# A state-space convolution and a token mixer on one core: another division of the convolution's work among the engines, four product buffers in its last step, and an order for each step

## The chip, the cores and the metric

The kernel runs on one core of one Trainium2 chip. A core has a matrix engine (TensorE, PE in the profile, whose weight loads are listed apart as PEld), a vector engine (VectorE, DVE), a scalar engine (ScalarE, ACT), a general engine (GpSimd, POOL) and an engine that here only issues transfers (SyncE, SP). Each works through its own instructions in program order and waits on semaphores for the others. The metric is the device time of one execution in microseconds, lower being better.

## The reference

The input u has 2048 positions of 512 channels. Two residual blocks follow each other, each on a layer norm of its input:

```python
def _A_ref(u, log_A_real, A_imag, C_real, C_imag, log_dt, D_skip):
    dt = jnp.exp(log_dt)
    A = -jnp.exp(log_A_real) + 1j * A_imag
    C = (C_real + 1j * C_imag) * dt[:, None]
    P = jnp.exp((A * dt[:, None])[:, :, None] * pos[None, None, :])
    K = 2.0 * jnp.einsum("dn,dnl->dl", C, P).real
    y = jnp.fft.irfft(jnp.fft.rfft(u_t, 2 * L) * jnp.fft.rfft(K, 2 * L), 2 * L)[:, :, :L]
    return y + u * D_skip
...
h = x + _A_ref(_layernorm(x), ...)
h2 = h + _B_ref(_layernorm(h), B_x, B_w1, B_w2, B_w3, B_w4)
```

The first block is a causal convolution of each channel with a kernel K of 2048 taps, which is a sum of 128 decaying oscillations. The second is a mixer: a layer norm, w1, a gelu, four shifts along the positions, w2, a residual, and then an MLP with w3 and w4.

## The kernel before, in words

There are two phases. `conv_phase` computes the first block, `mixer_phase` the second. The mixer's instructions stand in an order written out by hand; its layers 1 to 4 appear in the profile as matmuls into l, l3a to l3g and acc. The change doesn't touch the mixer.

**The convolution** goes in four steps s of 128 channels each (`WID`), and the channels in 32 chunks g of 16 (`CH`), eight to a step. For each chunk `table(g)` builds the taps as an outer form. Phases of the oscillations are integers that POOL adds up (`phases`, tile pt). ACT turns them into an absolute value, a sine and a cosine (three passes over 128 x 1056). The decays are tables: E (from eb) for the short distances, ec for multiples of 512, and from these amx (DVE, kept in PSUM, with or without squares by ACT) and amy, tile amp (an outer product of E and ec, on DVE or POOL). Six products of phases and decays give the tables cs and sn: four are always on DVE (with amx), and the last part of each, csy and sny (with amp), is on DVE or POOL. `taps(s, g)` multiplies cs and sn on PE, and ACT copies the taps to kt.

`spectra_of_taps` transforms the taps of a step: 64 channels at once with transposes on DVE (`stage_a_turn`) or 32 at a time with ACT copies (`stage_a_taps`). `stage_a_x` does the same for the normalised input. For each of eight parts e of the spectrum, `product(s, e)` then takes a matmul with the table tbs (`stage_b`), multiplies the spectra (DVE, or ACT and POOL in two halves) into a buffer u, and, where the lists say so, adds the four terms pairwise to two on DVE or POOL. `stage_b_inv(s, e)` transforms back with the table ms, from two terms if they were added and from four if not, and ACT copies the result to at. `stage_a_inv` turns a quarter of it on DVE into one of the same two buffers u, transforms it with fis and adds it to h. In the last step `last_a_inv` does that in place. The tables of step s+1 are built while the products of step s run; the last step has only its products. The input's spectra of steps 2 and 3 are made early and parked in DRAM (`FAR`, `spectrum_x`, `back`).

**The order** of all this is worked out before the program is emitted, by a list scheduler (`Plan`). Each operation is a node with an engine, an estimated cost, what it reads and writes, and a nominal due time `at`. `order()` walks through time and for each engine takes what can start first, breaking near ties by the due time that follows from the node's successors. The due times come from `NOM`, a dictionary of numbers, and from `TS`, one start for each step. So they act as priorities, not as times. Where `order()` expects PE to be idle for long it puts in filler matmuls of the identity (`busy`), as many as its model of the clock asks for; their results are not used.

**The division** among engines is `SHARE`. 'amy', 'csy', 'sny' list the chunks (modulo 8) whose part is on POOL, 'sq' those with squares on ACT, one list for step 0 and one for all others. 'turn' lists the groups of 64 channels that are transposed (only the first list is read), 'hadd' the halves of a step whose addition to h is done by PE (only the first is read; a group is 2s + r//2 with s up to 2), 'mul0' and 'mul2' the products on POOL, 'sum0' to 'sum3' the pairwise sums on DVE and on POOL. 'nrm' lists the tiles of the first layer norm that POOL normalises; of the others the first `LND` are DVE's and the rest ACT's. `LNA` tiles would have their statistics from ACT instead of DVE.

**The start.** `rates()` makes the decays with nine exponentials on ACT from one PSUM bank: six for eb at once, three for ec later, between two loads of the activation tables. `transpose(t)` brings the parameters of 128 channels into place, `params` prepares them, `norm_x` is the layer norm of the input.

## Time and profile before

| | |
|---|---|
| Median of 3 runs | 686.98 us (686.71 to 688.92) |
| The profiled execution | 687.03 us |
| Its span, first to last instruction | 685.2 us |
| Mean granted PE clock | 0.994 |
| Busy share of the span | PE 95%, PEld 74%, DVE 80%, ACT 59%, POOL 59% |
| First weight matmul of the mixer (l) | 305.4 us |

The page cuts the span into 40 equal slices; each digit is a busy share in tenths (the granted clock for PEclk):

```profile
PE   5987989999999997999999999999999999999997
DVE  5998898999898998999978798866879954455554
ACT  7889878867889876245634555544365443444330
POOL 1889589968999999002676219355635555554210
PEclk9998999999999999999999999999999999999999
```

The mixer begins in slice 18. Up to slice 16 three engines are near full at once; afterwards PE alone is. All instructions that were emitted through the scheduler or the ordering wrapper carry one line, L86, so groups are told apart by their tiles. A group's row gives the line, engine and operation, the tiles written and read, their shapes, the count, then busy time and mean ns, then idle time of the engine before them and what ended it. An f32 matmul appears as two records.

### The profile page before, as it was taken

The numbers are of one execution on the slowest core, as the hardware profiler recorded it, in microseconds if no ns is written. First come the engines' busy times: TensorE is split into PE (matmuls) and PEld (weight loads), VectorE is DVE, ScalarE is ACT, GpSimd is POOL, SyncE is SP. The second block draws the span as 40 slices with busy tenths as digits, with TensorE's granted clock in tenths as the row PEclk, the third lists the DMA queues.
The fourth block names the chain that finished last, engine by engine and source line by source line (L and its number), as shares of the span: only waits on it lengthen the run. The fifth ranks groups of instructions, "written<-read, shape, count | busy, mean of one in ns | idle before, by whom it ended". The sixth has DMA issues, their size and how long they took to land.

```text
span 685.2 us, 16971 instructions
## 1 busy us (share of the span) xinstructions
PE 649.8 (95%) x6898; PEld 509.3 (74%) x6898; DVE 547.8 (80%) x952; ACT 407.6 (59%) x706; POOL 405.3 (59%) x422
## 2 busy tenths in 40 slices
PE   5987989999999997999999999999999999999997
PEld 5984756663677684768888888888888888888885
DVE  5998898999898998999978798866879954455554
ACT  7889878867889876245634555544365443444330
POOL 1889589968999999002676219355635555554210
PEclk9998999999999999999999999999999999999999
DMA  8940644011201133020232311134311342211004
GB/s 204 255 163 2 186 156 110 3 48 33 64 3 49 34 96 109 1 64 1 61 94 51 104 32 48 45 90 113 101 36 50 101 127 62 61 47 47 22 10 123
DMA packets 49266, 51.50 MB, mean 75 GB/s; under 512 B 6436, under 2 KB 33060, under 8 KB 49188
## 3 DMA queue, kind: packets, MB, share of 16 engines
q1 hardware_dynamic: 47524, 47.80, 24.7%
q10 hardware_dynamic: 1152, 1.57, 0.9%
q0 software_dynamic: 512, 1.05, 0.6%
q8 instruction: 54, 0.88, 0.5%
q14 instruction: 24, 0.20, 0.1%
HBM read 35.72 MB, written 8.39 MB: 64 GB/s over the span
## 4 chain that ended last, share of the span: by engine, by line
PE 61%; DVE 14%; ACT 12%; DMA 4%; POOL 4%; issue 3%; SPq 1%; DVEq 0%; ACTq 0%; POOLq 0%
PE l L86 24%; PE acc L86 11%; ACT pt L86 7%; PE bank L86 6%; DVE u L86 4%; DVE at L86 3%; PE l3g L86 3%; PE l3d L86 3%; PE l3f L86 3%; PE l3e L86 3%; PE l3c L86 3%; PE l3b L86 3%; PE l3a L86 3%; DMA h<-in_A_u_dram 3%; DVE cs L86 2%
## 5 line engine op out<-in xcount | busy, mean ns | idle before, releaser
L86 ACT ACTIVATE pt<-pt 128x1056 f32<-128x1056 int32 x64 | 69.8, 1091 | 14.7 <-DVE cs L86 6.6
L86 POOL TENSOR_TENSOR pt<-p,s 128x512 int32<-128x512 int32 x64 | 72.4, 1148 | 4.5 <-DVE sn L86 3.3
L86 PE MATMUL bank<-at,tbs 128*64 128x128 f32 (+1 forms) x768 | 63.1, 311 | 3.3 <-DVE u L86 1.6
L86 PEld LDWEIGHTS bank<-at,tbs 128*64 128x64 f32 x768 | 44.6, 134 | 20.6 <-ACT at L86 3.0
L86 PEld LDWEIGHTS bank<-ident 128*128 128x128 f32 x418 | 50.5, 199 | 8.3 <-issue 5.1
L86 PE MATMUL bank<-ident 128*128 128x128 f32 x418 | 54.6, 287 | 0.0
L86 PE MATMUL bank<-u,ms 64*128 64x128 f32 x768 | 50.5, 280 | 3.5 <-DVE at L86 1.3
L86 PEld LDWEIGHTS bank<-u,ms 64*128 64x128 f32 x768 | 45.3, 187 | 8.3 <-issue 1.8
L86 POOL TENSOR_TENSOR cs0w<-raw,cs0w 128x512 fp32r<-128x512 f32 x7 | 9.1, 1294 | 58.9 <-ACT cs0w L86 58.9
L86 DVE TENSOR_TENSOR cs<-pt,amx 128x512 f32<-128x512 f32 x64 | 40.9, 678 | 2.4 <-ACT pt L86 1.2
L86 DVE TENSOR_TENSOR h<-h,l 128x512 f32<-128x512 f32 x48 | 32.1, 684 | 11.1 <-PE l L86 11.1
L86 PEld LDWEIGHTS bank<-cs 128*32 128x32 f32 x1024 | 24.2, 111 | 21.9 <-POOL cs L86 6.1
L86 POOL TENSOR_TENSOR sn1w<-raw,sn1w 128x512 fp32r<-128x512 f32 x7 | 9.5, 1361 | 52.2 <-ACT sn1w L86 52.2
L86 PE MATMUL bank<-cs 128*32 128x64 f32 x1024 | 32.7, 225 | 7.8 <-DVE cs L86 3.6
L86 DVE TENSOR_TENSOR u<-u,l3f 128x512 f32<-128x512 f32 x14 | 9.5, 682 | 36.9 <-PE l3f L86 36.9
L86 ACT COPY at<-bank 128x512 f32<-128x512 f32 x40 | 25.0, 631 | 22.6 <-PE bank L86 22.6
L86 ACT ACTIVATE pt<-pt,halfpi 128x1056 f32<-128x1056 f32 x32 | 38.1, 1190 | 0.5
L86 POOL TENSOR_TENSOR sn<-pt,amp 128x512 f32<-128x512 f32 x30 | 36.8, 1228 | 1.4 <-ACT pt L86 1.1
L86 DVE STREAM_TRANSPOSE at<-bank 128x512 f32<-128x512 f32 (+1 forms) x40 | 35.6, 919 | 2.0 <-PE bank L86 1.9
L86 ACT ACTIVATE u<-u 128x512 f32<-128x512 f32 x56 | 35.4, 632 | 1.8
L86 PE MATMUL bank<-sn 128*32 128x64 f32 x1024 | 32.0, 223 | 2.5 <-DVE sn L86 2.5
L86 POOL TENSOR_TENSOR cs<-pt,amp 128x512 f32<-128x512 f32 x26 | 31.9, 1225 | 3.5 <-PE bank L86 1.2
(1157 smaller groups left out, 2085.1 us busy)
## 6 DMA issues: line engine op xcount, KB each, us to landing
raw<-in_B_w_dram SPq DMA_DIRECT2D x28, 256.0 KB, 2.8
xq<-xq SPq DMA_DIRECT2D x72, 64.0 KB, 2.0
h<-in_A_u_dram SPq DMA_DIRECT2D x32, 128.0 KB, 4.3
h<-in_A_u_dram SPq DMA_DIRECT2D x16, 256.0 KB, 4.4
rawa<-in_B_w_dram SPq DMA_DIRECT2D x14, 256.0 KB, 2.9
rawb<-in_B_w_dram SPq DMA_DIRECT2D x14, 256.0 KB, 2.8
ms<-in_mm_dram SPq DMA_DIRECT2D x4, 768.0 KB, 10.5
out_dram<-h SPq DMA_DIRECT2D x48, 64.0 KB, 1.7
```

Source lines behind the costliest of these rows:

```text
L86: ins = f(*args, **kw)
```

## The change

Only the convolution is touched.

- The lists: 'amy', 'csy', 'sny' and 'sq' now have one entry for each step. On POOL stand afterwards 23 amy (19 before), 26 csy (26) and 24 sny (30); 24 chunks have squares on ACT (22). One group of step 1 (index 2) goes from `stage_a_turn` to two pairs of `stage_a_taps`. Step 0 adds up its terms for e = 4, 6 on POOL (before 1, 4, 6 on POOL and 3 on DVE), step 2 for 4 on DVE and 3, 6 on POOL (4, 5, 6 on POOL), step 3 for 0, 1, 4, 6, 7 on DVE and 2, 5 on POOL, and not for 3 (all on DVE). Product 4 of step 3 is POOL's.
- The first layer norm: POOL normalises no tile, DVE 0 to 3, ACT 4 to 15. The statistics of tiles 0 to 3 are ACT's, by two passes each with an accumulated sum.
- The decays: ec for 512 comes from an exponential right after the six for eb, that for 1024 is its square (ACT), that for 1536 the product of both (POOL). The second visit to the exponential's table is gone. The evacuation of block 0's parameters goes to DVE.
- The last step has four product buffers: the two u and the space of thp and ini, the parameters that no table needs any more by then.
- The due times: most entries of `NOM` have an addend for each step now (`nom`), each step's start `TS` has its own, all values are new, and two empty nodes stand for the norm that follows the convolution.

```diff
--- before.py
+++ after.py
@@ -21,20 +21,20 @@
...
-SHARE = {'nrm': [[1], [5]], 'mul0': [[0], [7]], 'mul2': [[6], []], 'amy': [[0, 1, 3, 4, 5, 6, 7], [1, 2, 3, 6]], 'csy': [[1, 4, 5, 6, 7], [0, 1, 2, 3, 4, 5, 7]], 'sny': [[1, 2, 3, 5, 6, 7], [0, 1, 2, 3, 4, 5, 6, 7]], 'sq': [[0, 1, 5, 7], [0, 2, 3, 4, 6, 7]], 'turn': [[1, 2, 3, 5, 6, 7], [2, 3, 5, 6, 7]], 'hadd': [[0, 1, 2, 7], [0, 1, 2, 3, 5, 6, 7]], 'sum0': [[3], [1, 4, 6]], 'sum1': [[], [0]], 'sum2': [[], [4, 5, 6]], 'sum3': [[0, 1, 2, 3, 4, 5, 6, 7], []]}
+SHARE = {'nrm': [[], []], 'mul0': [[2], [7]], 'mul2': [[7], [4]], 'amy': [[0, 1, 2, 3, 4, 5, 6, 7], [0, 1, 2, 3, 4], [0, 1, 2, 4, 7], [3, 4, 5, 6, 7]], 'csy': [[2, 3, 5, 6], [0, 1, 2, 3, 4, 5, 6, 7], [0, 1, 2, 3, 4, 5, 6, 7], [0, 1, 2, 4, 5, 7]], 'sny': [[1, 2, 3, 5, 6, 7], [1, 2, 4, 6, 7], [0, 1, 2, 4, 6], [0, 1, 2, 3, 4, 5, 6, 7]], 'sq': [[0, 1, 2, 6], [0, 2, 3, 4, 5, 6, 7], [1, 2, 3, 4, 5, 6, 7], [1, 3, 4, 5, 6, 7]], 'turn': [[1, 3, 5, 6, 7], [2, 3, 5, 6, 7]], 'hadd': [[0, 1, 2], [0, 1, 2, 3, 5, 6, 7]], 'sum0': [[], [4, 6]], 'sum1': [[], [0]], 'sum2': [[4], [3, 6]], 'sum3': [[0, 1, 4, 6, 7], [2, 5]]}
...
-LND = 5
-LNA = 0
+LND = 4
+LNA = 4
...
@@ -333,6 +333,8 @@
     TS = [NOM["t0"]]
     for w_ in WID:
         TS.append(TS[-1] + NOM["per"] * w_ / 128)
+    TS = [t + NOM.get(f"t.{i}", 0) for i, t in enumerate(TS)]
+    nom = lambda n, s: NOM[n] + NOM[f"{n}.{s}"]
...
-    decays += [(ec[:, :, k], 512.0 * k) for k in range(1, 4)]
+    decays += [(ec[:, :, 1], 512.0)]
...
-        for i, (d, m) in enumerate(decays[:6]):
-            add("ACT", 0.52, lambda d=d, m=m: act.activation(d, plan.view(p), AF.Exp, scale=-m), r=["lam"], w=["eb", ("exp", i)], at=-93)
-        sine = lambda: act.activation(tiny, halfpi, AF.Sin)
-        add("ACT", 1.45, sine, r=[("exp", i) for i in range(6)], w=["trig"], at=-92)
+        for i, (d, m) in enumerate(decays):
+            add("ACT", 0.99 if i == 6 else 0.52, lambda d=d, m=m: act.activation(d, plan.view(p), AF.Exp, scale=-m), r=["lam"],
+                w=["ex" if i == 6 else "eb", ("exp", i)], at=-93, frees=p if i == 6 else None)
+        add("ACT", 1.45, lambda: act.activation(tiny, halfpi, AF.Sin), r=[("exp", i) for i in range(7)], w=["trig"], at=-92)
 
         def rest():
-            for i, (d, m) in enumerate(decays[6:]):
-                add("ACT", 0.99 if i else 2.3, lambda d=d, m=m: act.activation(d, plan.view(p), AF.Exp, scale=-m), r=["lam"], w=["trig"], at=NOM["exp"])
-            add("ACT", 1.45, sine, w=["trig", "ex"], at=NOM["exp"], frees=p)
+            add("ACT", 0.99, lambda: act.activation(ec[:, :, 2], ec[:, :, 1], AF.Square), w=["ex"], at=NOM["exp"])
+            add("POOL", 1.2, lambda: gp.tensor_tensor(ec[:, :, 3], ec[:, :, 1], ec[:, :, 2], ALU.mult), w=["ex"], at=NOM["exp"])
...
+            if t:
+                act.activation(blk(thp, t, 1), chunked(b[:, 0:128]), AF.Copy, scale=1.0 / TWO_PI)
+            else:
+                v.tensor_scalar(blk(thp, t, 1), chunked(b[:, 0:128]), 1.0 / TWO_PI, None, ALU.mult)
+            copy = act.copy if t else v.tensor_copy
+            copy(am[:, t * 128 : t * 128 + 128], b[:, 128:256])
+            copy(blk(ini, t, 1), chunked(b[:, 256:384]))
+
+        add("ACT" if t else "DVE", 0.54 if t else 0.6, evac, r=[("prm", t)], w=[("A", t), ("C", t), ("I", t)], frees=p)
...
-        if g % 8 in SHARE["sq"][g >= 8]:
+        if g % 8 in SHARE["sq"][g // 8]:
...
-        pooled = lambda n: ("POOL", 1.04 if n == "amy" else 1.18, gp) if g % 8 in SHARE[n][g >= 8] else ("DVE", dve(CH * 32), v)
+        pooled = lambda n: ("POOL", 1.04 if n == "amy" else 1.18, gp) if g % 8 in SHARE[n][g // 8] else ("DVE", dve(CH * 32), v)
...
-        nominal = NOM["kg0"] + c * NOM["kgs0"] if s == 0 else TS[s - 1] + NOM["kg"] + c * NOM["kgs"] * WID[s - 1] / WID[s]
+        nominal = NOM["kg0"] + c * NOM["kgs0"] if s == 0 else TS[s - 1] + nom("kg", s) + c * nom("kgs", s) * WID[s - 1] / WID[s]
...
     g_ = [t.rearrange("p (d i t) -> p d i t", i=32, t=2) for t in uu]
+    uu += [t.rearrange("p g i d -> p (g i d)") for t in (thp, ini)]
+    PARAM = [("A", t) for t in R4] + [("I", t) for t in R4]
+
+    def turn_of(s, e):
+
+        k = e % (4 if s + 1 == NS else 2)
+        return uu[k], [("u", k)] + (PARAM if k > 1 else [])
...
-        u, uk = uu[e % 2], ("u", e % 2)
+        u, uk = turn_of(s, e)
...
-            add("ACT", 0.22 + n * 0.51e-3, lambda: act.copy(tap, taps_()), w=[uk], frees=p)
-            add("POOL", 3.0, pooled, r=keys, w=[uk, ("made", s, e)])
+            add("ACT", 0.22 + n * 0.51e-3, lambda: act.copy(tap, taps_()), w=uk, frees=p)
+            add("POOL", 3.0, pooled, r=keys, w=uk + [("made", s, e)])
         else:
-            add("DVE", 0.07 + 2 * n * 1.06e-3, mult, r=keys, w=[uk, ("made", s, e)], frees=p)
+            add("DVE", 0.07 + 2 * n * 1.06e-3, mult, r=keys, w=uk + [("made", s, e)], frees=p)
...
-        q = uu[e % 2][:, 0 : 2 * n].rearrange("p (i k d) -> p i k d", i=4, k=2)
+        u, uk = turn_of(s, e)
+        q = u[:, 0 : 2 * n].rearrange("p (i k d) -> p i k d", i=4, k=2)
...
-        a0 = 16 - LNA
-        for j in range(a0):
+        for j in range(LNA, 16):
             add("DVE", 0.6, lambda j=j: v.bn_stats(bx[:, j, :], h[:, j, :]),
                 r=[("x", j // 2, c) for c in R4], w=[("bs", j)])
-        for j in range(a0):
+        for j in range(LNA, 16):
             add("DVE", 0.08, lambda j=j: v.bn_aggr(mv[:, j, :], bx[:, j, :]), r=[("bs", j)], w=["mv"])
...
+            for j in range(LNA):
                 add("ACT", 0.62, lambda j=j: act.activation(junk, h[:, j, :], AF.Copy, accum_out=sm[:, j : j + 1]),
-                    r=[("x", j // 2, c) for c in R4], w=[("u", 0), "sm"])
...
+    add("DVE", 0.4, lambda: None, r=["part"], w=["mv"], at=TS[NS])
+    add("DVE", 2.75, lambda: None, r=["mv"], w=["norm"], at=TS[NS])
     plan.filler = busy
     plan.run()
```

In the same way as in `taps`, every `NOM` of 'kg', 'kgs', 'ak', 'ax', 'b', 'ib', 'y' and 'ys' is replaced by `nom` of that step.

46 lines of the change are left out of this document (21 added, 25 removed).

## The prediction

> **What bounds the kernel now.** I read the chain that ended last first (start, length, what), to see where the span is set.
>
> ```profile
> core 0 of [0], span 685.2 us
> 305.40 8.63 PE l L86 x36
> ...
> 675.33 5.45 PE l L86 x24
> ```
>
> From 305.4 us on the chain is TensorE (PE) alone, and the change touches nothing there: those 379.8 us stay. Whatever happens, happens in the convolution before 305.4. So I cut that part into stretches. The columns are length, then busy time (instructions) of PE, PEld, DVE, ACT and POOL, then the granted clock, DMA share and GB/s.
>
> ```profile
> 0.00:30.00 30.00, 22.27 (x174) 21.52 (x174) 22.90 (x71) 22.89 (x46) 13.59 (x25) 1.00 0.84 207
> 30.00:51.00 21.00, 18.07 (x320) 17.28 (x316) 19.96 (x43) 18.87 (x29) 18.06 (x18) 1.00 0.57 211
> 51.00:69.00 18.00, 14.15 (x284) 8.76 (x282) 15.30 (x22) 16.28 (x31) 17.91 (x16) 0.81 0.01 2
> 69.00:137.00 68.00, 63.24 (x1438) 45.33 (x1430) 62.39 (x104) 56.87 (x103) 56.76 (x57) 1.00 0.39 115
> 137.00:206.00 69.00, 64.57 (x1122) 40.22 (x1121) 65.72 (x105) 53.86 (x94) 57.20 (x60) 1.00 0.15 37
> 206.00:264.00 58.00, 53.51 (x1377) 40.09 (x1377) 52.22 (x74) 50.27 (x88) 55.49 (x53) 1.00 0.24 66
> 264.00:294.00 30.00, 28.30 (x414) 19.34 (x403) 27.42 (x42) 9.54 (x17) 9.52 (x8) 1.00 0.14 37
> ...
> 0.00:305.40 305.40, 274.38 (x5238) 199.61 (x5238) 276.18 (x484) 232.22 (x411) 228.54 (x231) 0.99 0.31 89
> ```
>
> PE looks fullest, but part of it is filler: matmuls of the identity that carry no result. The same view of the tile ident alone (PE, PEld, POOL):
>
> ```profile
> 69.00:137.00 68.00, 5.30 (x38) 4.54 (x38) 0.00 (x0) 1.00 0.39 115
> 137.00:206.00 69.00, 10.25 (x50) 6.18 (x50) 0.00 (x0) 1.00 0.15 37
> 206.00:264.00 58.00, 5.28 (x24) 3.05 (x24) 0.00 (x0) 1.00 0.24 66
> 264.00:294.00 30.00, 2.29 (x15) 1.90 (x16) 0.00 (x0) 1.00 0.14 37
> ```
>
> Taken off, PE's own work is 57.9 of 68 us, 54.3 of 69, 48.2 of 58 and 26.0 of 30, against 62.4, 65.7, 52.2 and 27.4 on DVE. DVE is the bound in three of these stretches; between 206 and 264 POOL (55.5) is a little above it. From 30 to 264 DVE is idle for 18.4 us in all (lengths less busy time: 1.0, 2.7, 5.6, 3.3, 5.8). Work taken off DVE should therefore come out nearly whole, unless PE or POOL is next.
>
> **The change part by part.** The rows for DVE, with busy time and mean ns of one, then idle time before it and its releasers:
>
> ```profile
> L86 DVE TENSOR_TENSOR u<-xs,bank 128x1024 f32<-128x1024 f32 x23 | 27.6, 1214 | 0.8 <-ACT xs L86 0.6
> L86 DVE TENSOR_TENSOR sn<-pt,amx 128x512 f32<-128x512 f32 x32 | 21.7, 679 | 3.8 <-ACT pt L86 1.5 <-POOL h L86 1.3 <-ACT amx L86 0.5
> L86 DVE STREAM_TRANSPOSE at<-bank 128x512 f32<-128x512 f32 x24 | 16.0, 697 | 0.0
> L86 DVE TENSOR_TENSOR amx<-E,amx 128x512 f32<-128x512 f32 x22 | 15.1, 686 | 5.8 <-ACT amx L86 5.6
> L86 DVE TENSOR_TENSOR amx<-E,amx 128x896 f32<-128x896 f32 x10 | 11.0, 1098 | 2.7 <-ACT amx L86 2.7
> L86 DVE BATCH_NORM_STATS2 bs<-h 128x6 f32<-128x512 f32 x16 | 10.5, 666 | 0.0
> L86 DVE TENSOR_TENSOR amp<-E,ec 128x512 f32<-128x512 f32 x13 | 10.2, 788 | 0.1
> L86 DVE TENSOR_TENSOR u<-u 128x256 f32<-128x256 f32 x18 | 7.7, 470 | 0.3
> L86 DVE TENSOR_TENSOR cs<-pt,amp 128x512 f32<-128x512 f32 x6 | 6.5, 1079 | 0.0
> L86 DVE TENSOR_TENSOR sn<-pt,amp 128x512 f32<-128x512 f32 x2 | 2.2, 1118 | 0.0
> L86 DVE TENSOR_SCALAR scratch<-scratch 128x128 f32<-128x128 f32 x4 | 0.9, 220 | 0.1
> ```
>
> The new lists move the following on DVE, stage by stage.
>
> The tables of step 0 (0 to about 69 us): four tiles' statistics go to ACT, 4 x 0.666 = -2.66 (their short aggregates are left aside); one amp more goes to POOL, -0.79; one cs comes back, +1.08; the three evacuations of block 0 come from ACT. No row shows those three on DVE; 0.22 each as the nearest row, twice that as the other end: +0.7. Sum -1.7.
>
> The tables of step 1, with the products of step 0: amp -0.79, cs -1.08, three sn back at +1.12 = +3.35, one more chunk that squares on ACT -0.41 (1.098 - 0.686), one pair of sums (e=3) gone, -0.94, and one group of tap spectra built without transposes, 4 x 0.697 = -2.79. Sum -2.7.
>
> The tables of step 2: -0.79 - 1.08 + 3.35 - 0.41 = +1.1. Of step 3: amp -0.79, cs +1.08, a pair of sums from POOL +0.94 = +1.2. The products of step 3: one product to POOL, -1.21, three pairs of sums gone from DVE, -2.82, together -4.0. In step 2 the pooled product is only another one, and the extra index 7 in the old list hadd has no group (indices end at 5), so its removal does nothing.
>
> The price of sn is the soft one: 0.68 (the same size with an operand amx) to 1.12; I take 1.12, the row of the operation itself. At 0.68 the whole would be 2.6 us better.
>
> The last step is not DVE's alone. Its PE work, first and last row of PE's timeline between the first product and the first matmul of what follows:
>
> ```profile
> 275.95 1.10 PE L86 MATMUL bank<-at,tbs 128*64 128x128 f32 x16
> ...
> 293.91 0.59 PE L86 MATMUL bank<-h,ident 128*128 128x512 f32 x1
> ```
>
> That is 18.0 us, of which at most 2.3 us were filler. And PE gains work from the lists; these rows price it:
>
> ```profile
> L86 PE MATMUL bank<-u,ms 64*128 64x128 f32 x768 | 50.5, 280 | 3.5 <-DVE at L86 1.3 <-DVE u L86 1.2 <-POOL u L86 0.6
> L86 PE MATMUL bank<-kt,fas 32*32 32x512 f32 x192 | 11.8, 600 | 1.9 <-DVE at L86 1.6 <-ACT at L86 0.3
> L86 PE MATMUL bank<-fas,kt 32*64 32x32 f32 x512 | 8.7, 219 | 0.0
> ```
>
> A product without its sums needs 16 more of the first row, 16 x 50.5/768 = 1.05: two in step 0, one in the last. The group that is no longer transposed goes from 11.8/6 = 1.97 to 8.7/2 = 4.35, +2.4. So PE's own work becomes 57.9 + 2.1 + 2.4 = 62.4 of 68 in the stretch from 69 us (it still fits), and 26.0 + 1.05 = 27.05 of 30 in the last. The last stretch can give at most 30 - 27.05 = 2.95. What would let it give so much are the four buffers: now steps 2's transposes hold both u, and the first product (273.5) waits for them. If the products still start where they do, PE needs 18.0 - 2.3 + 1.05 = 16.75 from there, a gain of 1.2. Between the two I take 2.0.
>
> POOL and ACT:
>
> ```profile
> L86 POOL TENSOR_TENSOR sn<-pt,amp 128x512 f32<-128x512 f32 x30 | 36.8, 1228 | 1.4 <-ACT pt L86 1.1 <-POOL pt L86 0.2
> L86 POOL TENSOR_TENSOR amp<-E,ec 128x512 f32<-128x512 f32 x19 | 21.4, 1130 | 5.5 <-DVE ec L86 5.1
> L86 POOL TENSOR_SCALAR h<-h,mvh,bs 128x512 f32<-128x512 f32 x2 | 4.1, 2070 | 0.0
> L86 ACT ACTIVATE h<-h,bs 128x512 f32<-128x512 f32 x10 | 7.4, 800 | 0.0
> L86 ACT ACT_TABLE_LOAD x4 | 5.1, 1283 | 0.8 <-PEq L1640 0.7
> L86 ACT ACTIVATE ec<-bank 128x512 f32<-128x512 f32 x3 | 3.2, 1150 | 0.0
> ```
>
> POOL loses two normalised tiles (-4.14) and six sn (-7.37), gains four amp (+4.52), a product in two halves (about two sn, +2.46) and the cube of the decay (about an amp, +1.1): -3.4 in all. Normalising on POOL also made DVE wait once, 1.3 us (the sn row above); with no tile on POOL I take that off: -1.3.
>
> ACT at the start: two exponentials become one square (-1.15), and the return to the exponential's table goes (two loads, -2.57). It gains eight passes for the statistics. No row has one with an accumulated sum; 8 x 0.80 = +6.4 as the nearest, plus two tiles to normalise, +1.6. The net, about +4.3, meets 7.1 + 2.1 us of ACT idle time before 51 us, so I cost it at nothing; if these passes stand ahead of the first tables' sines in ACT's order, it costs the part that the loads don't pay back, 6.4 - 3.7 = 2.7.
>
> **The sum.** -1.7 - 2.7 + 1.1 + 1.2 - 2.0 - 1.3 = -5.4, and 687.03 (the profiled execution, 1.8 us over its span of 685.2; the median of the runs, 686.98, is the same) becomes 681.6. Ends: with the last stretch at 2.95 and sn at 0.68, -9.0 (678.0); with 1.2 there and ACT's 2.7 paid, -1.9 (685.1). The new priorities are costed at nothing for themselves: they decide the rivals.
>
> **The rivals.**
>
> *The order also takes DVE's waits.* Each step gets its own numbers. If half of the 18.4 us of idle time goes too, 681.6 - 9.2 = 672.4. For it: the idle time is in many small waits of about 1 us. Against: PE, at 62.4 of 68, leaves little in one stretch, POOL in another.
>
> *The last step gives nothing more, because POOL's two pairs of sums stand in DVE's way.* DVE's cs with amp takes 1.079 while POOL is at work, against 0.68 with amx, which lies in PSUM. If the last step stays as it is (0 for 2.0, and e=3 costs its 1.05), 687.03 - 3.4 + 1.05 = 684.7. For it, in a page's words: the Trainium skill, "SBUF — State Buffer", Who interferes with whom, says that a DVE instruction with two SBUF inputs contends with a GpSimd one that reads SBUF, one of them blocking for its whole length. These rows agree. Against: DVE falls to 14 of 18 us there (18.0 less 4.0), so it has room.
>
> *ACT takes DVE's place.*
>
> ```profile
> DVE amx L86 <- ACT amx L86: 8.3, 13, 1.2
> ```
>
> This wait (us, times, longest) is DVE's largest, and ACT gets more in its way. If it grows by two thirds, 5.5 us, the gain is gone: 687.1. Against: ACT has 11 to 15 us free in each stretch from 69 to 206.
>
> *PE's clock drops in more places, and the kernel is slower.* Between 51 and 69 us PE ran at a mean of 0.81 (the windows above):
>
> ```profile
> 59.69 0.46 PE L86 MATMUL bank<-sn 128*32 128x64 f32 x8
> ...
> 65.72 0.28 PE L86 MATMUL bank<-sn 128*32 128x64 f32 x8
> ```
>
> The same eight matmuls take 0.46 there and 0.28 after. With the three sn on DVE and all eight cs on POOL in steps 1 and 2, a group's last product may come later than now. At 0.81 the stretch from 69 needs 62.4/0.81 = 77.0 (+9.0), that from 206 needs 48.2/0.81 = 59.5 (+1.5), that from 137 still fits (67.0). Kept: the start (-1.7 - 1.3) and the end (-2.0). 687.03 + 10.5 - 5.0 = 692.5. It decides from a mean clock of 62.4/68 = 0.92 down. Against: fillers were planned into the gaps and only one stretch shows it. The Trainium skill, "TensorE: Matmul & The Clock Gate", What's actually happening, has the clock halved after an idle window of some 3.4 us, until a busy one; by it a single gap costs an estimated 1.7 us, and six would be needed.
>
> **How the numbers follow.** The forecast, 681.6: 0.38, its own range 678.0 to 685.1. The waits taken too, 672.4: 0.22. The last step unchanged, 684.7: 0.10. ACT in DVE's place, 687.1: 0.12. The clock, 692.5: 0.18. A measurement of this kernel can't tell from no change what lies within 0.3%, 684.9 to 689.0. The first two cases lie below (0.60), half of the third (0.05) and a little of the fourth (0.02): faster 0.67. The other half of the third and the rest of the fourth are the same, 0.15; the clock is slower, 0.18. The range runs from 669 to 692; the outer parts of the second case and of the last are left out, some 0.1 each.
>
> **What would show it.** DVE busy 270 us before layer 1 (276.2 up to 305.4 now, less 6.1); the first l matmul near 300 instead of 305.4; two table loads fewer; no POOL operation on h before 69 us; sn with amp on DVE x8, still near 1.1; the first product of the last step before the last transpose of step 2 into u. It would be wrong if the first l matmul came no earlier than 303.5, with a granted clock under 0.92 in a stretch (the clock) or a larger wait of DVE for amx (ACT), or if it came before 296 (the waits).

## The result and the profile after

| | before | after |
|---|---|---|
| Median of 13 runs each | 687.77 us (686.51 to 689.15) | 685.92 us (685.17 to 686.45) |
| Ratio | | 0.9971, 95% interval 0.9962 to 0.998 |
| The profiled execution, its span | 687.03, 685.2 us | 685.61, 683.8 us |
| First matmul of layer 1 | 305.40 us | 304.28 us |

The change makes the kernel 0.29% faster, about 2 us, where 5.4 us (681.6) were forecast. Below, "the changed kernel" is this one, and a time against it is worked out from two ratios to the kernel before: (ratio - 0.9971) x 687.5 us.

Lines of the page of the changed kernel: the span, the busy times, and the granted PE clock in 40 slices.

```profile
span 683.8 us, 17275 instructions
...
PE 640.7 (94%) x7044; PEld 501.6 (73%) x7044; DVE 549.2 (80%) x938; ACT 414.5 (61%) x729; POOL 403.6 (59%) x421
...
PEclk9996999999999999999999999999999999999999
```

One slice has a low clock, as before, and all else looks alike: at this scale the two can't be told apart. So I cut both at the same events: the end of DVE's last cosine product with amx of a step's eighth chunk (the row of the timeline below ends at 81.6 us; 152.7, 210.2 and 264.7 are the ends in the next steps), and the first matmul of layer 1.

```profile
80.39 1.27 DVE L86 TENSOR_TENSOR cs<-pt,amx 128x512 f32<-128x512 f32 x2
```

Busy times between these events, columns as in the prediction: before,

```profile
0.00:75.80 75.80, 61.30 (x900) 53.52 (x900) 64.47 (x142) 64.29 (x116) 54.72 (x62) 0.95 0.55 155
75.80:150.40 74.60, 69.33 (x1502) 48.63 (x1500) 69.47 (x127) 58.30 (x106) 59.45 (x61) 1.00 0.33 98
150.40:207.80 57.40, 53.48 (x987) 32.20 (x986) 54.05 (x78) 47.93 (x84) 51.15 (x52) 1.00 0.14 34
207.80:263.60 55.80, 51.49 (x1288) 38.59 (x1288) 50.10 (x72) 48.11 (x85) 53.30 (x52) 1.00 0.25 69
263.60:305.40 41.80, 38.79 (x566) 26.67 (x566) 38.09 (x72) 13.59 (x24) 9.92 (x8) 1.00 0.18 53
```

and after:

```profile
0.00:81.60 81.60, 56.57 (x926) 47.92 (x926) 70.70 (x149) 69.20 (x134) 51.41 (x60) 0.90 0.53 154
81.60:152.70 71.10, 65.57 (x1500) 45.91 (x1500) 67.35 (x114) 57.63 (x105) 56.94 (x58) 1.00 0.32 95
152.70:210.20 57.50, 53.84 (x1104) 33.06 (x1098) 54.38 (x76) 50.73 (x91) 52.81 (x52) 1.00 0.15 35
210.20:264.70 54.50, 52.35 (x1302) 39.38 (x1298) 51.34 (x73) 47.88 (x83) 51.52 (x50) 1.00 0.21 66
264.70:304.28 39.58, 37.29 (x566) 25.48 (x562) 33.78 (x64) 13.60 (x24) 14.52 (x13) 1.00 0.17 55
0.00:304.28 304.28, 265.61 (x5384) 191.75 (x5384) 277.55 (x470) 239.05 (x434) 227.20 (x230) 0.97 0.31 89
```

| stretch | predicted change | measured |
|---|---|---|
| tables of step 0 | -3.0 (-1.7 and the wait -1.3) | +5.8 |
| tables of step 1 | -2.7 | -3.5 |
| tables of step 2 | +1.1 | +0.1 |
| tables of step 3 | +1.2 | -1.3 |
| last step, up to layer 1 | -2.0 | -2.2 |
| sum | -5.4 | -1.1 |

(The spans of the two profiled executions differ by 1.4 us, the medians by 1.85; what is more than 1.1 lies behind the first l or in the spread of the runs.) By 152.7 us the changed kernel is 2.3 us late instead of 5.7 early. DVE's busy time before layer 1 went from 276.18 to 277.55, not to 270; its idle time from 29.2 (305.40 - 276.18) to 26.7. The groups tell why the busy time didn't fall. DVE after, up to 304.28 us, mean ns of one behind the comma:

```profile
L86 DVE TENSOR_TENSOR amp<-E,ec 128x512 f32<-128x512 f32 x9 | 8.3, 919 | 0.0
L86 DVE TENSOR_TENSOR sn<-pt,amp 128x512 f32<-128x512 f32 x8 | 7.6, 944 | 0.6 <-ACT pt L86 0.6
L86 DVE TENSOR_TENSOR cs<-pt,amp 128x512 f32<-128x512 f32 x6 | 7.1, 1181 | 0.0
L86 DVE SCALAR_TENSOR_TENSOR scratch<-scratch 128x128 f32<-128x128 f32 x14 | 5.2, 369 | 0.2
L86 DVE TENSOR_TENSOR scratch<-scratch 128x128 f32<-128x128 f32 x10 | 4.4, 465 | 0.1
L86 DVE SCALAR_TENSOR_TENSOR scratch<-scratch 128x256 f32<-128x256 f32 x7 | 4.1, 591 | 0.0
```

and three of these before (amp and the products with amp stand in the prediction):

```profile
L86 DVE SCALAR_TENSOR_TENSOR scratch<-scratch 128x128 f32<-128x128 f32 x14 | 3.9, 282 | 0.1
L86 DVE SCALAR_TENSOR_TENSOR scratch<-scratch 128x256 f32<-128x256 f32 x7 | 2.9, 420 | 0.0
L86 DVE TENSOR_TENSOR scratch<-scratch 128x128 f32<-128x128 f32 x10 | 2.7, 286 | 0.1
```

The same ten operations on scratch take 465 ns each for 286. I summed this over every group of DVE's: the new counts at the old durations make 6.7 us less (6.1 were forecast), the longer durations 8.6 us more. About 6 of the 8.6 lie in instructions that read two operands from SBUF, as those shown here do; the rest is spread over transposes, normalisations and others. The Trainium skill, "SBUF — State Buffer", Who interferes with whom, has such an instruction contend with a GpSimd one that reads SBUF. The rows fit it, since nothing about the operations on scratch was changed but when they run.

In the first table stretch the +5.8 is DVE's busy time: it grew by 6.2 us there (64.47 to 70.70), while its idle time hardly changed (11.3 to 10.9). By the same sum over that stretch's groups, longer durations make 4.9 us. Another part is only moved: nine of the scratch TENSOR_TENSOR lie in it for six before, and two reciprocals for one. By these and their neighbours some 3 us of the next block's parameters were done earlier; they are missing in the second stretch.

In the last step the products begin earlier. PE's timeline, first product and first matmul of what follows, after:

```profile
272.19 1.99 PE L86 MATMUL bank<-at,tbs 128*64 128x128 f32 x32
...
292.54 1.88 PE L86 MATMUL bank<-h,ident 128*128 128x512 f32 x4
```

and the first product before:

```profile
273.51 1.10 PE L86 MATMUL bank<-at,tbs 128*64 128x128 f32 x16
```

From the first product to the first of the others it takes 20.35 us (20.40 before): PE needs as long as it did. But the products begin 7.5 us after the tables' end (264.7) and not 9.9 (263.6): this is the whole gain. What made them begin earlier is read from the runs below.

### The profile page after: what moved, and what is told of

Same layout as the page of the kernel before. It is cut to its first block, busy times and chain, and to the rows that moved or that the text cites. A ratio compares the mean times of both kernels' runs of the same rounds, so it can differ in the third digit from the quotient of the medians.

```text
span 683.8 us, 17275 instructions
## 1 busy us (share of the span) xinstructions
PE 640.7 (94%) x7044; PEld 501.6 (73%) x7044; DVE 549.2 (80%) x938; ACT 414.5 (61%) x729; POOL 403.6 (59%) x421
## 3 DMA queue, kind: packets, MB, share of 16 engines
q1 hardware_dynamic: 47524, 47.80, 24.3%
## 4 chain that ended last, share of the span: by engine, by line
PE 65%; DVE 12%; ACT 10%; POOL 5%; issue 3%; DMA 3%; SPq 1%; POOLq 0%; ACTq 0%; DVEq 0%
PE l L86 24%; PE acc L86 11%; PE bank L86 10%; ACT pt L86 6%; DVE cs L86 3%; PE l3b L86 3%; PE l3a L86 3%; PE l3g L86 3%; PE l3d L86 3%; PE l3f L86 3%; PE l3e L86 3%; PE l3c L86 3%; DVE sn L86 2%; DMA h<-in_A_u_dram 2%; POOL pt L86 2%
## 5 line engine op out<-in xcount | busy, mean ns | idle before, releaser
L86 PE MATMUL bank<-u,ms 64*128 64x128 f32 x736 | 47.5, 278 | 5.8 <-DVE u L86 2.2
L86 PEld LDWEIGHTS bank<-u,ms 64*128 64x128 f32 x736 | 43.1, 188 | 9.7 <-DVE u L86 2.9
L86 PE MATMUL bank<-ident 128*128 128x128 f32 x292 | 39.8, 294 | 0.0
L86 ACT COPY at<-bank 128x512 f32<-128x512 f32 x44 | 27.0, 625 | 20.0 <-PE bank L86 18.8
L86 PEld LDWEIGHTS bank<-ident 128*128 128x128 f32 x292 | 36.7, 204 | 2.9 <-DVE at L86 1.1
L86 DVE STREAM_TRANSPOSE at<-bank 128x512 f32<-128x512 f32 (+1 forms) x36 | 33.0, 959 | 1.6 <-PE bank L86 1.4
L86 POOL TENSOR_TENSOR sn<-pt,amp 128x512 f32<-128x512 f32 x24 | 29.5, 1228 | 5.1 <-issue 3.9
```

The lines of the kernel that those rows point to most:

```text
L86: ins = f(*args, **kw)
```

## The experiments

Letters name theories within one expectation; the same letter may mean another thing in the next. A run "in the same order" emits every operation at its place in the changed kernel's order and alters only the operation itself. Stretches are named by their measured end or length, as above.

| run | ratio, interval | against the changed kernel | step 0 ends | step 1 ends | last step |
|---|---|---|---|---|---|
| changed kernel | 0.9971 | | 81.6 | 152.7 | 39.6 |
| e1_two_buffers | 1.0033, 1.002 to 1.0046 | +4.3 | 80.9 | 151.6 | 44.0 |
| e2_old_last | 1.001, 1.0 to 1.002 | +2.7 | 81.4 | 152.5 | 43.0 |
| e12_before_last_step | 1.0078, 1.0064 to 1.0092 | +7.4 | 75.9 | 150.4 | 45.8 |
| e10_old_order_new_lists | 1.0252, 1.0235 to 1.0269 | +19.3 | 77.5 | 155.4 | 43.0 |
| e11_new_order_old_lists | 1.0152, 1.0136 to 1.0167 | +12.4 | 82.2 | 154.8 | 39.6 |
| e3_stats_on_dve | 0.9996, 0.9988 to 1.0005 | +1.7 | 83.1 | 154.3 | 39.6 |
| e8_two_loads | 0.9996, 0.9988 to 1.0005 | +1.7 | 83.1 | 153.8 | 39.6 |
| e5_no_norm_act | 0.995, 0.9937 to 0.9963 | -1.4 | 81.0 | 152.1 | 39.6 |
| e9_norm_pool | 0.9979, 0.9971 to 0.9988 | +0.5 | 81.7 | 152.3 | 39.7 |
| e7_kt_first | 1.0053, 1.0041 to 1.0066 | +5.6 | 86.2 | 156.8 | 39.6 |
| e13_short_dve | 0.9905, 0.989 to 0.9919 | -4.5 | 79.6 | 148.1 | 39.7 |
| e14_short_pool | 0.9957, 0.9945 to 0.9969 | -1.0 | 80.7 | 150.9 | 39.7 |
| e15_short_act | 0.9969, 0.9943 to 0.9995 | -0.1 | 81.8 | 150.9 | 39.7 |
| e16_norm_later | 0.9982, 0.9974 to 0.9991 | +0.8 | 81.7 | 152.3 | 39.7 |
| e17_root_later | 1.0039, 1.0027 to 1.0052 | +4.7 | 86.0 | 157.1 | 39.6 |
| e18_root_norm_later | 1.0039, 1.0026 to 1.0053 | +4.7 | 85.8 | 156.6 | 39.6 |

Two runs that read operands from PSUM (e4, e6) are told below without stretches.

**The last step, in parts.** Two buffers instead of four (the order is the same up to the first product of that step and is planned anew behind it):

```diff
-        k = e % (4 if s + 1 == NS else 2)
+        k = e % 2
```

> The changed kernel with two product buffers in the last step instead of four; the emitted order is the same up to the last step. Theory A (the last step, 2.2 us shorter from the last chunk's table to layer 1, owes that to the buffers): the stretch grows again by 2 us or more, 688 us against 685.9 of the changed kernel, a ratio to before of about 1.000. Rival (the new lists did it, the buffers are idle help): within 0.5 us of the changed kernel, ratio 0.997.

Four buffers, but the old lists of that step:

```diff
-'mul2': [[7], [4]], ... 'sum3': [[0, 1, 4, 6, 7], [2, 5]]
+'mul2': [[7], []], ... 'sum3': [[0, 1, 2, 3, 4, 5, 6, 7], []]
```

> The changed kernel with the old lists in the last step alone (all eight products on VectorE, all eight pairs of sums on VectorE), four buffers kept; same order up to there. VectorE gets its 4.0 us back there. Theory A (buffers): less than 1 us slower than the changed kernel. Rival (lists): 2 us slower or more, ratio to before about 1.000. If TensorE's own work decides the last step, it is not slower at all, since TensorE has 1 us less to do.

The kernel before with both, and with its own order numbers (its first four stretches are those of before):

```diff
-'mul2': [[6], []], ... 'sum3': [[0, 1, 2, 3, 4, 5, 6, 7], []]
+'mul2': [[6], [4]], ... 'sum3': [[0, 1, 4, 6, 7], [2, 5]]
...
+    uu += [t.rearrange("p g i d -> p (g i d)") for t in (thp, ini)]
...
+        k = e % (4 if s + 1 == NS else 2)
```

> The kernel before, the same up to the last step, with that step's four product buffers and its new lists (sums of five products on DVE and two on POOL, one more product on POOL); no other part of the change. If the last step's gain stands by itself, its stretch falls from 41.8 to the changed kernel's 39.6 or near it, and the whole is 2 to 2.5 us faster than before, at least as fast as the whole change: the rest of the change (start, lists, new order) is then worth nothing. If it hangs on the new order of the last step, less than 1 us.

The last window without the lists:

```profile
264.40:307.38 42.98, 39.38 (x562) 27.44 (x559) 37.47 (x71) 13.06 (x24) 9.03 (x7) 0.96 0.17 51
```

The last window of the kernel before with buffers and lists:

```profile
263.60:309.44 45.84, 40.95 (x603) 29.75 (x603) 34.96 (x65) 14.00 (x25) 15.33 (x14) 1.00 0.17 48
```

Before it was 41.8 us, and the whole change has 39.6. Any two of the parts without the third are slower than none of them: without the buffers 44.0, without the lists 43.0, without the new order 45.8. The gain of 2.2 belongs to the three together, and a price for one of them alone has no meaning here. (In all three runs the plan of the step is made anew, so that its order and its fillers differ, too.)

The earlier start of the products isn't the buffers'. PE's timeline with two buffers, first product:

```profile
271.18 1.10 PE L86 MATMUL bank<-at,tbs 128*64 128x128 f32 x16
```

With four buffers and the lists, but in the old order, the first product is this:

```profile
273.62 1.10 PE L86 MATMUL bank<-at,tbs 128*64 128x128 f32 x16
```

The tables end at 263.65 us in both. So with two buffers the products start after 7.5 us, as in the changed kernel, and with four in the old order after 10.0, as before: the early start came with the new order. What grows when a part is missing is the time from the first product to the first of the others: 20.35 us in the changed kernel, 24.7 with two buffers (271.18 to 295.87), 23.7 with the old lists (271.98 to 295.64), 24.3 in the old order (273.62 to 297.92).

**Lists against order, in the table work.** The order of one kernel, with the engines of amp, of the third cs and sn and of the squares by the lists of the other:

```diff
...
-        add(e1, c1, lambda: eng1.tensor_tensor(sny, pv[:, 1, :, 0:32], amy, ALU.mult), r=[ky, kp], w=[ksn + (2,)], port=True)
+        add(e1, c1, lambda: on("sny").tensor_tensor(sny, pv[:, 1, :, 0:32], amy, ALU.mult), r=[ky, kp], w=[ksn + (2,)], port=True)
...
```

> The kernel before with every step in its old order, only the engines of the table work (amp, the third cs and sn, the squares) by the new lists. By the prediction's prices the lists alone cost DVE 0.3 us in step 0, 1.1 in step 1, 1.1 in step 2 and 0.3 in step 3. Theory O (the new order of the start lost the 8 us, not the lists): the tables of step 0 end within 1.5 us of before's 75.8 and those of step 1 within 2 of 150.4; the whole is within 3 us of before. Rival L (the lists load an engine too much): the tables of step 0 end at 79 or later.

> The changed kernel with every step in its new order, only the engines of the table work (amp, the third cs and sn, the squares) by the old lists. Theory O (the order of the start lost the time): the tables of step 0 still end within 1.5 us of the changed kernel's 81.6, those of step 1 within 2 of 152.7. Rival L (the lists): they end at 78 or earlier. In steps 2 and 3, whose order and lists were chosen together, old lists in the new order should be 1 to 4 us slower by theory W (each engine's queue waits for the others), 2 us faster by the prediction's prices.

By the prices of the prediction the lists differ by 3 us of DVE at most. Measured: the old order loses 17 us by the new lists (1.0252), the new order 12 by the old ones. Neither theory stands: the new lists in the old order end step 0 at 77.5, but step 1 at 155.4, 5 us late; and the new order keeps its late step 0 with either lists (82.2), so that this lateness is the order's or of what else the start has that is new. Steps 2 and 3 show what is lost, by the busy times from 154.8 to 275.3 with the old lists in the new order,

```profile
154.80:275.30 120.50, 108.11 (x2396) 73.36 (x2396) 105.39 (x146) 98.59 (x171) 101.53 (x101) 0.99 0.17 46
```

and in the changed kernel:

```profile
152.70:264.70 112.00, 106.18 (x2404) 72.44 (x2396) 105.72 (x147) 98.61 (x173) 104.33 (x101) 1.00 0.18 50
```

DVE, ACT and POOL are no busier in the slower one, and yet it is 8.5 us longer. All of it is waiting. The waits of this stretch in the slower one (us, times, longest):

```profile
ACT pt L86 <- DVE cs L86: 6.6, 6, 2.3
POOL pt L86 <- DVE sn L86: 6.6, 5, 2.6
...
DVE cs L86 <- ACT amx L86: 4.3, 4, 1.9
```

In the changed kernel the first two are 3.1 and 2.4, the last 1.2. ACT can't build the next phases before DVE has used the last, POOL can't before DVE's product, DVE can't before ACT's squares: a list and an order that were not made for each other put someone at the head of each queue whose partner comes late.

**What an engine's time is worth.** In the same order, work was made shorter and no wait was added: DVE's products with amp from chunk 3 on a quarter of their rows, and its parameter work of the later blocks on a quarter of its columns,

```diff
-            lambda: v.tensor_tensor(mx, ma, mb, ALU.max),
+            lambda: v.tensor_tensor(Mx, Ma, Mb, ALU.max),
...
+        part = lambda e, w: w[:, 0:4] if e is v and g > 2 else w
...
```

> The changed kernel with every instruction and every wait in its place, but DVE's two-input operations that grow beside POOL made short: its products with amp from chunk 3 on a quarter of their rows, the parameter work of the blocks after the first on a quarter of its columns (the rest of the tables then keeps older values). About 15 to 20 us of DVE's work before layer 1 are gone and no new wait for ACT's amx comes in. The prediction's rule (what is taken off DVE comes out nearly whole): the first matmul of layer 1 comes 12 to 18 us before the changed kernel's 304.3. Theory W (the three engines wait for each other in turn): it comes 2 to 6 us earlier.

POOL's amp and its products with amp on a quarter (`e is gp`),

> The changed kernel with every instruction and every wait in its place, but POOL's amp and its products with amp, from chunk 3, on a quarter of their rows (the tables keep older values there): 45 to 55 us of POOL's work are gone, and DVE's operations beside it should shorten as in the run with operands from PSUM. Rule of the prediction (POOL is not the bound, but for 206 to 264 us): 4 to 10 us earlier at the first matmul of layer 1, as DVE's shorter durations and the stretch from 206 us make. If POOL is the engine whose latency the chain runs through (phases, then ACT's sine, then products): 15 us or more.

and ACT's absolute values over a quarter:

```diff
-        add("ACT", 0.97, lambda: act.activation(tc_, pi, AF.Abs), r=[kp], w=[kc])
+        add("ACT", 0.97, lambda: act.activation(tc_[:, 0 : NP // (4 if g > 2 else 1)], pi[:, 0 : NP // (4 if g > 2 else 1)], AF.Abs), r=[kp], w=[kc])
```

> The changed kernel with every instruction and every wait in its place, but ACT's absolute values of the phases, from chunk 3, over a quarter of their columns (the cosine tables keep older values there): 18 to 22 us of ACT's work are gone. The prediction (ACT hidden behind its idle time): within 2 us of the changed kernel. Theory W: 3 to 8 us earlier at the first matmul of layer 1. If ACT is the engine that all wait for: 12 us or more.

The window up to the first l, with DVE's work short:

```profile
0.00:299.01 299.01, 263.69 (x5384) 191.21 (x5384) 266.37 (x470) 238.79 (x434) 222.70 (x230) 0.98 0.31 91
```

With POOL's work short:

```profile
0.00:302.39 302.39, 265.08 (x5385) 191.36 (x5385) 270.89 (x470) 238.66 (x434) 178.55 (x230) 0.98 0.31 90
```

With ACT's:

```profile
0.00:301.35 301.35, 264.82 (x5384) 191.55 (x5385) 278.47 (x470) 222.10 (x434) 227.78 (x230) 0.97 0.31 90
```

11.2 us less of DVE (277.55 to 266.37) bring the first l 5.3 us forward (304.28 to 299.01): 0.47 of each. 48.7 us less of POOL bring 1.9, and DVE is 6.7 us shorter there besides, since less stands in its way. 17.0 us less of ACT bring 2.9 in the profiled execution, 0.17 of each; the times of this run scatter from 682.5 to 691.2 us, so that its ratio says little. Of the three, DVE's time counts most, and less than half of what was taken off it counts. In step 3 none of the first two moved the 54.5 us, where PE is busy for 52.35.

The same question with the second operand in PSUM (amx, in place of amp and scratch), first in the changed kernel, then in the kernel before:

```diff
-            lambda: v.tensor_tensor(mx, ma, mb, ALU.max),
+            lambda: v.tensor_tensor(mx, ma, other(mb), ALU.max),
...
```

> The changed kernel in its emitted order; VectorE's products with amp (14) and the operations with two inputs in the preparation of parameter blocks 1 to 3 take their second input from the PSUM tile amx instead, so the decays of those products and the parameters of channels 128 to 511 are not the reference's. Instructions and sizes are the same. Theory C (these operations wait inside themselves for GpSimd's): VectorE's products with amp fall from 0.94 and 1.18 to 0.68 us, the parameter operations of 128 elements from 0.47 to 0.3, VectorE's busy time before layer 1 falls by 8 us or more, and the time by 3 to 7 us, ratio about 0.990. Theory S (ScalarE): durations may fall, the time by less than 1 us, ratio 0.996 or more.

> The kernel before, in its order, with the second operand of DVE's products with amp, and of its parameter work of the later blocks, read from amx in PSUM and not from SBUF (so these values aren't the reference's): DVE's instructions with two SBUF inputs no longer grow beside POOL. DVE's busy time before layer 1 should fall by 5 to 7 us (six cs from 1.08 to 0.68, two sn from 1.12 to 0.68, some thirty operations on scratch, amounts by the same replacement in the changed kernel). The prediction's rule (work taken off DVE comes out nearly whole): 4 to 6 us faster than before. Theory W (the three engines wait for each other in turn, and time freed on one of them becomes its own idle time): within 1.5 us of before.

In the changed kernel, groups of DVE up to the first l:

```profile
L86 DVE TENSOR_TENSOR sn<-pt,amx 128x512 f32<-128x512 f32 x40 | 27.2, 680 | 5.9 <-ACT amx L86 2.6 <-POOL cs L86 1.5 <-ACT pt L86 0.6
...
L86 DVE SCALAR_TENSOR_TENSOR scratch<-scratch,amx 128x256 f32<-128x256 f32 x7 | 2.9, 414 | 0.3 <-ACT amx L86 0.3
```

591 became 414 and the products with amp 680 like the others: here the growth goes with the second operand in SBUF. DVE's busy time fell by 10.9 us to 266.65, and the kernel became no faster: 0.9992 (0.9983 to 1.0001), 1.4 us above the changed kernel. But here every such operation reads amx, so that ACT must wait with the next amx, and the waits for it grew (2.6 us before sn alone). So this run doesn't say what the 10.9 us are worth; the one with short operations does. In the kernel before, DVE lost 3.9 us (276.18 to 272.29; 5 to 7 expected) and the kernel gained 0.1% (0.9989, 0.998 to 0.9998): not the 4 us of the prediction's rule. But there the waits for ACT's amx grew as well (9.8 us before amx, for 8.3), so that this run doesn't price DVE's time alone either.

**ACT and POOL at the start.** All in the same order. Statistics of the first four tiles back on DVE:

```diff
-                add("ACT", 0.62, lambda j=j: act.activation(junk, h[:, j, :], AF.Copy, accum_out=sm[:, j : j + 1]),
+                add("ACT", 0.62, lambda j=j: v.bn_stats(bx[:, j, :], h[:, j, :]),
...
```

> The changed kernel in its emitted order, but the statistics of the first four tiles are made by VectorE at the places in the order where ScalarE's passes stood. ScalarE loses some 6 us of work before 30 us, VectorE gains 3.3. Theory S (ScalarE's passes delay the start): the eighth chunk's table ends 2 us or more earlier than the 81.6 us of the changed kernel, and the time falls by 1 to 3 us, ratio about 0.994. Theory C (VectorE's longer operations are the loss, ScalarE's passes are not): 1 to 3 us slower, ratio about 1.000.

Two table loads put back around the square of the decays:

```diff
+                act.activation(tiny, halfpi, AF.Exp)
                 act.activation(ec[:, :, 2], ec[:, :, 1], AF.Square)
+                act.activation(tiny, halfpi, AF.Sin)
```

> The changed kernel with two table loads put back around the square of the high decays: a tiny exponential before it, a tiny sine behind it, so 2 x 1.28 plus two short activations, about 3.0 us more of ACT's work at 14 to 18 us. The prediction (ACT at the start hides behind its own idle time, costed at nothing): the tables of step 0 end within 0.5 us of 81.6 and the whole within 0.7 us. Theory A (ACT binds the start): they end 2 to 3 us later, and the whole is 1.5 to 3 us slower than the changed kernel; the change would have been no faster than before without that part.

ACT's twelve normalisations left out:

```diff
-                add("ACT", 0.71, lambda j=j: act.activation(
-                    h[:, j, :], h[:, j, :], AF.Identity, scale=rs[:, j : j + 1], bias=nb[:, j : j + 1]),
+                add("ACT", 0.71, lambda: None,
```

> The changed kernel with every instruction in its order, but without ScalarE's (ACT's) twelve normalisations of x (tiles 4 to 15 of h stay as loaded, so the result isn't the reference's); 12 x 0.80 = 9.6 us of ACT's work between 37 and 57 us are gone. Theory A (ACT binds the start: between 45 and 57 us of the changed kernel it is busy 11.9 of 12 us, VectorE (DVE) 8.7): the tables of step 0 end 3 to 5 us before the changed kernel's 81.6, since DVE's 3.3 us of idle time there go and then DVE is the bound; the whole comes out 2 to 4 us faster than the changed kernel. Theory D (DVE's longer instructions alone set the pace): 81.6 within 0.7, and no change of the whole beyond 1 us.

Two of them on POOL (`gp.tensor_scalar` for tiles 8 and 13):

> The changed kernel with two of ACT's twelve normalisations (tiles 8 and 13) done by GpSimd (POOL) at the same places of the order, as two tiles were before: ACT loses 1.6 us, POOL gains 2 x 2.07 = 4.1 us. Theory A (ACT is the only bound at the start): the tables of step 0 end about 1 us before 81.6. Rival (the chain goes from POOL's phases to ACT's sines, so POOL's time counts as much): they end 1 to 3 us after 81.6, and the whole is 0.5 to 2 us slower than the changed kernel, which would bear out the prediction's 1.3 us for taking POOL out of the normalisation.

Both the statistics and the loads end step 0 1.5 us later (83.1) and cost 1.7 us in all: moving the statistics to ACT gained this, and 3 us of ACT's time at 14 us cost half of it, not nothing. The normalisations, 8.4 us of ACT's time between 37 and 57 us, gave 0.6 at the end of step 0, though ACT is busy there nearly throughout. Without them it stood and waited; ACT's timeline of that run:

```profile
47.90 1.09 ACT L86 ACTIVATE pt<-pt 128x1056 f32<-128x1056 int32 x1 [2.66 <-DVE cs L86]
```

A full engine is not the bound if it only fills the time until its partner is ready. Two tiles on POOL made 0.1 us at step 0's end: what POOL's normalising was priced at, 1.3 us, isn't there.

**PE's gap at 50 us.** PE's timeline in the changed kernel:

```profile
48.19 0.29 PE L86 MATMUL bank<-sn 128*32 128x64 f32 x8
...
56.01 0.44 PE L86 MATMUL bank<-cs 128*32 128x64 f32 x8 [5.66 <-ACT kt L86]
56.19 0.47 PE L86 MATMUL bank<-sn 128*32 128x64 f32 x8
```

After 5.66 us without work the eight matmuls take 0.47 us and not 0.29, and do so until 65.8. By the Trainium skill, "TensorE: Matmul & The Clock Gate", What's actually happening, an idle window of about 3.4 us halves the clock; the trace agrees. The bank that PE waits for is freed by a copy of ACT's that stands behind three normalisations. So I moved these copies ahead:

```diff
+        for k, p in self.early:
+            order.remove(k)
+            order.insert(order.index(p) + 1, k)
...
+        if s == 0:
+            plan.early.append((kc, p))
```

> The changed kernel, with ACT's copies of the taps of step 0 out of PSUM (kt) moved ahead in ACT's order, each to right behind the matmuls that it copies; nothing else changes. In the changed kernel the copy of chunk 2 stands behind three normalisations until 55.66 us, TensorE (PE) waits 5.66 us for the bank, and then runs at half clock until 69 us. Theory C (this gap and the clock cost time): PE's wait at 50 to 56 us falls under 2 us, the granted clock in 51 to 69 us rises from 0.6 to over 0.9, and the kernel is 1 to 3 us faster than the changed one. Theory A (ACT's work is the bound, PE's gap only follows from it): the clock may rise, but the tables of step 0 end within 0.7 us of 81.6 and the whole is within 1 us of the changed kernel.

It became 5.6 us slower, and 4.6 of it stand already at the end of step 0 (86.2). ACT now waits for PE in front of these copies, up to that point (us, times, longest),

```profile
ACT kt L86 <- PE bank L86: 5.2, 6, 1.6
```

with the sines of the next chunk behind each. And PE's gap is no shorter; the wait for the bank has only become one for DVE:

```profile
58.24 0.44 PE L86 MATMUL bank<-cs 128*32 128x64 f32 x8 [6.45 <-DVE cs L86]
```

In the changed kernel, too, DVE's last cosine product for these matmuls ends at 55.83 us, just before they start at 56.01: an earlier copy couldn't have brought them forward. So this run doesn't price the gap, and what half clock alone costs there wasn't tried.

**The order at the start.** DVE's four normalisations behind chunk 2's products; then the thirteen operations of the root of the variances behind chunk 1's (with ACT's first four normalisations behind chunk 3's sines, and the root in SBUF), without and with the former:

```diff
+        behind(self.mark[0], [k for k in order if k in self.roots])
...
+        behind(self.mark[1], [k for k in order if k in self.own])
...
-        root = lambda: plan.view(first)[:, 0:16]
+        root = lambda: bs[:, :, 1, 3]
```

> The changed kernel with DVE's four normalisations of x (3.5 us from 41.5 us on) moved in DVE's order from ahead of chunk 2's products to right behind them, and nothing else. Theory O (the start lost its time to what stands ahead of the products in DVE's queue): chunk 2's products end 3 us before the changed kernel's 47.8, the normalisations fall into the 2.86 us that DVE waits for amx at 49 to 52 us, and the tables of step 0 end 1.5 to 3 us before 81.6; the whole gains 1 to 3 us on the changed kernel and is the fastest of all. If another queue sets the next chunk (ACT's or POOL's): within 0.7 us.

> The changed kernel, with the root of the variances (thirteen short operations of DVE, 3.6 us from 33.4 us on) moved in DVE's order from ahead of chunk 1's products to behind them, as it nearly stood before the change, its root kept in SBUF; ACT's first four normalisations, which need it, move behind chunk 3's sines. Theory O (the start lost its time to what stands ahead of the products in DVE's queue): chunk 1's products (38.2 us in the changed kernel) come 3 to 3.6 us earlier, and, since ACT can't begin chunk 2 before DVE has done chunk 1's last cosine product, so does chunk 2's part on ACT; DVE's own four normalisations still stand ahead of chunk 2's products, so that those gain 0 to 1 us. The tables of step 0 end 0 to 1.5 us before 81.6. If the start hangs on another engine: within 0.7 us.

> As the run before, and DVE's four normalisations also moved behind chunk 2's products. Theory O: chunk 1's and chunk 2's products come 3 to 3.6 us earlier than in the changed kernel (38.2 and 46.5 us), the tables of step 0 end 2 to 4 us before 81.6, and the whole is 2 to 4 us faster than the changed kernel, the fastest of all. Rival (ACT's normalisations, now later and closer together, hold up chunk 4 and 5 by as much): chunk 2 comes earlier, but the tables of step 0 end within 1 us of 81.6.

The first changed nothing at the end of step 0 (81.7). DVE's timeline shows that the normalisations had lain in a wait, which is left without them:

```profile
45.19 0.69 DVE L86 TENSOR_TENSOR sn<-pt,amx 128x512 f32<-128x512 f32 x1 [3.75 <-ACT amx L86]
```

The other two were 4.7 us slower, where theory O expected the last to be 2 to 4 us faster. They don't settle it, since they made the root itself longer. DVE's timeline with both moved:

```profile
35.88 0.69 DVE L86 TENSOR_TENSOR sn<-pt,amx 128x512 f32<-128x512 f32 x1 [2.27 <-ACT pt L86]
...
42.59 2.20 DVE L86 SCALAR_TENSOR_TENSOR bs<-bs 128x16 f32<-128x16 f32 x2
```

Chunk 1 comes only 1.1 us earlier (from 36.98), since ACT's sines are not ready; and the root, now with both operands in SBUF, takes 6.4 us (39.8 to 46.2) for 3.6, with two short operations of 2.20 us together. These 2.8 us are most of the 4.2 by which step 0 ends later. Then amx, and all that waits for it, comes late.

Where the lateness begins can be read further back, but wasn't tried. In DVE's order before:

```profile
22.86 0.70 DVE L86 TENSOR_TENSOR ec<-ec 128x384 f32<-128x384 f32 x1
...
29.04 0.68 DVE L86 TENSOR_TENSOR cs<-pt,amp 128x512 f32<-128x512 f32 x1
```

and after:

```profile
27.69 0.55 DVE L86 TENSOR_TENSOR ec<-ec 128x384 f32<-128x384 f32 x1
...
31.91 1.55 DVE L86 TENSOR_TENSOR cs<-pt,amp 128x512 f32<-128x512 f32 x1
```

The decays' product stands behind statistics, 4.8 us later; amp of chunk 0 needs it, its last cosine product ends at 33.46 instead of 29.72, and ACT can't begin chunk 1 before that. This 3.7 us is nearly the lateness of chunk 2 (4.3). No run was faster than the changed kernel that computed all that it computes.

## Why the prediction was right or wrong, point by point

**The step that failed** is the rule on which the sum rests: "Work taken off DVE should therefore come out nearly whole", with the durations of the rows of the kernel before. Both halves of it are wrong. The durations belong to the order: counts alone took 6.7 us off DVE, near the 6.1 that were forecast, but the same rows took 8.6 us more in the new order, 4.9 of them in the tables of step 0. DVE's busy time rose by 1.4 us; the kernel could still be faster because DVE's idle time fell by 2.5. And the exchange, where work was made shorter with no wait added, is 0.47 and not 1: DVE's idle time had been taken for the whole slack, but the waits shown above go in a circle, DVE's on ACT, ACT's and POOL's on DVE.

**Tables of step 0, -1.7 and -1.3.** The statistics went and the evacuations came as priced; the stretch grew by 5.8, which is some 3 of work moved ahead and 4.9 of longer durations, less what was taken off. POOL's normalising, -1.3, is worth nothing when put back. The lateness stays with the new order whichever lists are used. With most of DVE's growing operations made short, step 0 still ends at 79.6, for 75.8 before; the first cause is not settled.

**ACT's +4.3 at nothing.** It was to hide in ACT's idle time of 7.1 and 2.1 us (and left out that block 0's three evacuations leave ACT). Where it was tried, 3.0 us cost 1.5 to 1.7. The alternative given, that the passes for the statistics cost if they stand ahead of the first sines, gave ACT's part alone, 2.7. Together with what the statistics save on DVE, moving them gains 1.7 where they stand, four of the eight ahead of the first sines. The passes themselves, priced at 6.4, take 6.9 us: four of 629 ns, four of 718, and behind each an ACTIVATION_READ_ACCUMULATOR of 186 to 189 ns, which reads the sum.

**Steps 1 to 3, -2.7, +1.1, +1.2.** They came out at -3.5, +0.1, -1.3. Steps 2 and 3 are better than the lists' price; step 1 is so only by the 3 us that were done ahead, and without them it falls short of it. The prices were of lists alone; the run with the old lists in the new order shows that lists and order are one choice. The new lists put more work on DVE in steps 2 and 3 and were meant to; what they bought is fewer waits, which was one of the rivals (the order takes DVE's waits too). In the four table stretches DVE's idle time fell from 25.5 to 20.9 us, half of the 9.2 given; in the last step it rose by 2.1.

**The last step, -2.0.** Measured -2.2, but the agreement is luck. The mechanism named was that four buffers let the products start before the last transpose into u. The first product does start before it (272.19; the transpose is at 273.24), but so it does with two buffers (271.18; 272.16), and with four in the old order it doesn't (273.62; 272.82). The other part of the price, less work for PE, isn't there: the 18.0 us were read from 275.95, which is the second product; from the first (273.51) it was 20.40, and it is 20.35 now.

**sn at 1.12.** It is 0.944 on average; 0.68 was the other end.

**The other rivals.** POOL's sums in DVE's way at the end: they weren't, the step gave its 2.2. ACT in DVE's place: DVE's wait for ACT's amx shrank from 8.3 to 5.1 us. The clock: it fell deeper where it had fallen before (0.62 for 0.81 between 51 and 69 us) and a little ahead of that (0.92 for 1.00 between 30 and 51), and is 1.00 in every later stretch before layer 1, so the stretch from 69 us didn't become longer by it. Of the signs that were to show the forecast wrong, the first l after 303.5 came true, with such a clock in one stretch. What this clock cost at the start no run tells: with the copies first it was 0.75 there, but ACT's new waits came with it.

## What to carry to other kernels

Where several engines hand small pieces to each other in turn, the busiest one's time can be worth a fraction of itself: measure that fraction by shortening its operations in place, with no wait added, before adding up a change from durations. A division of work and the order made for it are one change; half of it can cost many times what the whole gains. A queue that is full may only be filling a wait, and taking its work away then shows little but the wait. A wait can have a second one right behind it: before removing what ended last, look when the other inputs were ready.

## What the runs showed of the hardware

An operation of DVE that takes 0.68 us with one operand in PSUM took 0.68 to 1.6 us with both in SBUF, in the same kernel, and one of 16 elements a partition 0.19 to 1.1; with the second operand of the products moved to PSUM the spread was gone. A second SBUF operand isn't needed for it: DVE's normalisations (128x512, one wide operand) took 0.53 to 1.42 us in the changed kernel, and 0.53 to 0.62 where POOL's work was short. Each pass of ACT that sums along the row brings a second instruction of 0.19 us. Two table loads of 1.28 us, with the two tiny activations that cause them, cost ACT 3.0 us and nothing besides: the next activation starts as the load ends.
